# Second set-aside score of ordinary turns moved up by half a row, between two parts of a filling product

## The chip, the core and the metric

The kernel runs on one core of one Trainium2 chip. The metric is the device time of one execution in microseconds (us). Engines are named TensorE (PE, its weight loads PEld), VectorE (DVE), ScalarE (ACT), GpSimd (POOL) and SyncE (SP).

## The reference

One sequence of 2048 rows with 512 features is normalised by layer norm. From it come an attention with 32 heads of 16 and a feed-forward layer of width 1792 with squared ReLU; the output is the input plus the product of both, the second through a SiLU.

```python
xn = layernorm(x)                                # 2048 x 512
q, k, v = split(xn @ wqkv, 32 heads of 16)
p = softmax(q @ k.T / 4)                         # 32 x 2048 x 2048
s = (p @ v) @ wo
h = relu(xn @ w1 + b1) ** 2                      # 2048 x 1792
g = silu(h @ w2 + b2)
out = x + s * g
```

All of it is wanted in float32 accuracy.

## The kernel before

After a start of about 150 us, in which the rows are normalised and queries, keys and values are made, the kernel runs 128 *turns* of much the same shape, and then a short tail. A turn handles four steps; a step is four heads, 512 queries and 128 keys. Its work per step:

- scores: for each pair of heads `p` two products of 64 contraction rows, which lie on rows 0 to 63 (*half 0*, `hp` = 0) and 64 to 127 (*half 1*, `hp` = 1) of TensorE. The two halves work side by side, into different banks of PSUM.
- the exponential of the scores by ScalarE (`exps`, L286), from PSUM into an SBUF tile P.
- `values` (L538): P times the values, 16 products of 32 columns for a turn, all at the end of the turn.

The scores of three of the four steps go into one of two buffers S of two banks each (`scores`), and ScalarE reads them there. The fourth step, `i + 3`, has no such buffer: each of its four scores goes alone into a single bank, `single` (tile name `lin`), VectorE copies it to P (`aside`, L305), and ScalarE takes the exponential in place in P later. These are the four *set-aside scores* of a turn. They come as `aside(i + 3, 0, 0)`, `(0, 1)`, `(1, 0)` and `(1, 1)`; the first and third lie on half 0, the second and fourth on half 1. There is one bank for all of them.

Between the scores TensorE is given *filling products*, the matrices of the feed-forward layer and, in the last sixteen turns, of the projection `wo`. A `Block` (tile name `spare`, L330) is a sum of twelve (at the end some of nine) products in each half, with a list `todo` for each half and a counter `at`. A pair of blocks is worked on at a time: in a turn one block gets the rows of half 0 and the other those of half 1, and `swap` exchanges them, so that a block is done after two turns. `lin(0, 1)` issues the next filling product of both halves, `lin(0)` or `lin(1)` that of one half; the latter stand beside a set-aside score, which occupies the other half. Eight of the 128 turns make and end a pair of blocks in one turn (`make and end`) and have an order of their own. The other 120 are the *ordinary* turns.

The order on each engine is written out by hand in the loop over turns (L754 on); there is no scheduler. In an ordinary turn TensorE is given: S scores; score 1 beside a filling product of half 1; S scores; four filling products on both halves; score 2 beside a filling product of half 0; S scores; two filling products on both; S scores; score 3 beside one of half 1; two on both; S scores of the next turn's first step; two on both; score 4 beside one of half 0; S scores; the products of `values`. All products before `values` have 512 columns.

Of the kernel before, what the change touches and what calls it, by code (L numbers as in the profile page):

```python
# [73 lines left out]
def fast_path(tc, sb, ps, env):  # L74
# [6 lines left out]
    mm = nc.tensor.matmul  # L81
# [4 lines left out]
    def t(shape, dt, tag):  # L86

        cnt[0] += 1
        p = ps if tag in ("S", "lin", "acc") else sb
        if tag in BUFS:  # L90
            turn[tag] = turn.get(tag, -1) + 1
            n = turn[tag] % BUFS[tag]
            tag = f"{tag}{places[n] if tag == 'S' else n}"
        return p.tile(shape, dt, tag=tag, name=f"{tag}_{cnt[0]}")
# [183 lines left out]
    def score(i, p, hp, dst):  # L278
        qd, qc, kb = steps[i]
        k, q = ka[qd, kb // 8], qa[qd, qc]  # L280
        r = slice(64 * hp, 64 * hp + 64)
        mm(dst, k[r, p, 128 * (kb % 8):128 * (kb % 8) + 128], q[r, p], start=True, stop=True)  # L282

    def exps(i, p, src):
        if src is not None:
            act.activation(ptile[i, p], src, AF.Exp, scale=SCALE)  # L286

    def place(i, p):
        ptile[i, p] = t([128, 2, 512], FT, f"P{2 * ((i - 1) % 4) + p}")

    def scores(i, p):

        if i < len(steps):
            sc = t([128, 2, 512], FT, "S")
            place(i, p)
            for hp in range(2):
                score(i, p, hp, sc[:, hp])
            return sc

    def aside(i, p, hp):  # L300

        if hp == 0:
            place(i, p)
        score(i, p, hp, single)
        dve.tensor_copy(ptile[i, p][:, hp], single)  # L305
# [5 lines left out]
    class Block:  # L311
# [10 lines left out]
        def issue(self, half, bank):  # L322
# [8 lines left out]
               stop=n == len(self.todo[half]) - 1 and self.at[other] > 0)  # L331
            return True

    pair, swapped = [None], [0]

    def lin(*halves):
        if pair[0]:  # L340
            for half in halves:
                j = half ^ swapped[0]
                pair[0][j].issue(half, lin_banks[j])

    def swap():
        if pair[0]:
            while any([pair[0][half ^ swapped[0]].issue(half, lin_banks[half ^ swapped[0]]) for half in range(2)]):
                pass
            swapped[0] ^= 1
            if not swapped[0]:  # L350
                pair[0][0].evict()
                pair[0] = None
# [21 lines left out]
    def split_piece(eng=None):  # L374
        if at_piece[1] == len(pieces):
            return
        j, layer, m = pieces[at_piece[1]]
        at_piece[1] += 1
        raw, q = raws.pop(0), PAIRS[m][1]
        wf[layer, m] = [t([128, 4, 256] if layer == 1 else [128, 2, 512], FR, f"wf{layer}{p}{q}") for p in "hl"]  # L380
        split(*wf[layer, m], raw, eng or dve, pool)
        load_piece()
# [15 lines left out]
    def second(c, g, i):  # L398
        ms = [m for m in range(len(PAIRS)) if PAIRS[m][0] == g]
        h, w = [hid[m] for m in ms], [wf[2, m] for m in ms]  # L400

        def evict():
            if g == 0:
                y[c, i] = t([128, 2, 512], FT, f"y{i}")
            old = b2b.unsqueeze(1).broadcast_to([128, 2, 512]) if g == 0 else y[c, i]
            dve.tensor_tensor(y[c, i], spare, old, op=OP.add)
            if g == 3:
                complete.add((c, i))

        return [Block(lambda p, k, j=j: h[k // 2][p][:, k % 2, 128 * j:128 * j + 128],  # L410
                      lambda p, k: w[k // 2][p][:, k % 2], range(2 * len(ms)), evict)
                for j in (2 * i, 2 * i + 1)]
# [8 lines left out]
    for c in ORDER:  # L421
        for m, (g, _) in enumerate(PAIRS):
            fill += [(lambda m=m: first(m), False), (None, True)]
            if m in (1, 2, 4, 6):
                for i in range(2):
                    make = lambda c=c, g=g if m > 1 else 0, i=i: second(c, g, i)
# [9 lines left out]
    for i in range(4):  # L436
        part = vt[:, 4 * i:4 * i + 4]
# [94 lines left out]
    def values(i):  # L532
        qd, qc, kb = steps[i]
        if kb == 0:
            acc[0] = t([128, 512], FT, "acc")
        for j in (1, 2, 3, 0) if i % 2 else (0, 1, 2, 3):
            o = (4 * qd + j) * 17
            mm(acc[0][32 * j:32 * j + 32], vt[:, kb, o:o + 32], ptile[i, j // 2][:, j % 2],  # L538
               start=kb == 0, stop=kb == NK - 1)

    def finish(i):

        qd, qc, kb = steps[i]
        if kb < NK - 1:
            return
        if i == len(steps) - 1:
            return
        ou = t([128, 512], FT, "ou")
        cast(act if turn_ends_first[0] else dve, ou, acc[0])
        sp.dma_start(zdram[qd][qc], ou[16::32])  # L550
        for j in range(4):
            sp.dma_start(udram[qd // 2][qc][0, qd % 2, :, j], ou[32 * j:32 * j + 16])
        n = i // 4
        events.setdefault(2 * n + 2, []).insert(0, (load_sums, (qd, qc)))
        at(n + 2, rowsums, qd, qc)
# [174 lines left out]
    def happen(time):  # L730
        for fn, a in events.pop(int(2 * time), ()):
            fn(*a)


    n = turn["S"]
# [3 lines left out]
    lin_banks = [spare[:, 0], spare[:, 1]]  # L739
# [3 lines left out]
    def rest(i, dst):  # L743

        group(dst, lambda p: onorm[2, 3][p][:, cut[i]], lambda p: wos[0][p][:, 3])

    def end_rest(i, src):

        o = t([128, 512], FT, f"wf2{'hl'[i // 2]}{i % 2}")
        dve.scalar_tensor_tensor(o, src, 0.5, gsb[2, i // 2][:, i % 2], op0=OP.mult, op1=OP.mult)  # L750
        pool.dma_start(out[1024 + 128 * i:1152 + 128 * i], o, accum_op=OP.add)

    turn_ends_first = [False]
    for n in range(TURNS):  # L754
        i = 4 * n
        happen(n)
        make, end, split_now = fill[n]
        if make:
            pair[0] = make()
        exps(i + 1, 0, scores(i + 1, 0))  # L760
        aside(i + 3, 0, 0)
        lin(1)
        exps(i + 1, 1, scores(i + 1, 1))
        for _ in range(5 if make and end else 4):
            lin(0, 1)
        if make and end:
            lin(0)
            aside(i + 3, 0, 1)
            exps(i + 2, 0, scores(i + 2, 0))
            swap()  # L770
            exps(i + 2, 1, scores(i + 2, 1))
            aside(i + 3, 1, 0)
            lin(1)
            exps(i + 3, 0, ptile[i + 3, 0])
            lin(0, 1)
            last = [scores(i + 4, 0)]
            for _ in range(4):
                lin(0, 1)
        else:
            lin(0)  # L780
            aside(i + 3, 0, 1)
            exps(i + 2, 0, scores(i + 2, 0))
            lin(0, 1)
            lin(0, 1)
            exps(i + 2, 1, scores(i + 2, 1))
            aside(i + 3, 1, 0)
            lin(1)
            exps(i + 3, 0, ptile[i + 3, 0])
            lin(0, 1)
            lin(0, 1)  # L790
            last = [scores(i + 4, 0)]
            lin(0, 1)
            lin(0, 1)
        lin(0)
        aside(i + 3, 1, 1)
        exps(i + 3, 1, ptile[i + 3, 1])
        last.append(scores(i + 4, 1))
        for p in range(2):
            exps(i + 4, p, last[p])
        if n == TURNS - 1:  # L800
            two = t([128, 2, 512], FT, "S")
            rest(0, two[:, 0])
        turn_ends_first[0] = n < LAST and end and fill[n][0] is None and fill[n - 1][2] and n % per in (7, 15, 23)
        swap()
        if n == LAST - 1:
            gsb.update({(2, i): y[2, i] for i in range(2)})
        if n == TURNS - 1:
            end_rest(0, two[:, 0])
        happen(n + 0.5)
        if split_now:  # L810
            split_piece()
        for j in range(4):
            values(i + j)
        finish(i + 3)
# [5 lines left out]
    zc, r = t([128, 16], FT, "zc"), t([128, 16], FT, "rc")  # L820
# [3 lines left out]
    half = [slice(0, 256), slice(256, 512)]  # L824
# [11 lines left out]
    for i in range(4):  # L836
        for j in range(4):
            mm(small[32 * j:32 * j + 32, 0, cut[i]], r[:, 4 * i + j:4 * i + j + 1].broadcast_to([128, 32]), ident,
               start=True, stop=True)
# [19 lines left out]
    for j in range(2):  # L859
        for todo in ((0, 0), (0, 1)), ((1, 0),):  # L860
            for i in (2 * j, 2 * j + 1):
                group(lins[i], lambda p: (h, l)[p][:, cut[i]], lambda p: wlast[0][:, p],
                      start=len(todo) == 2, stop=len(todo) == 1, todo=todo)
# [120 lines left out]
```

## Time and profile before

| | us |
|---|---|
| median of 3 runs | 1272.64 (1272.08 to 1272.99) |
| profiled execution, its own time | 1271.87 |
| span of the profile | 1270.1 |
| TensorE busy | 1257.2 |
| ScalarE busy | 1034.1 |
| VectorE busy | 678.0 |

The granted clock of TensorE is 0.997 over the span. In the rows, L282 is the score's product (tiles S or lin), L286 the exponential, L305 VectorE's copy of a set-aside score, L330 a filling product, L538 the product with the values. "64*128 64x512" is a product of 64 rows into 128 columns of TensorE, 512 columns long. A weight load (PEld) stands as an instruction of its own before each product. The recorded ends of products are modelled, so distances between starts say more than durations.

### The profile page before, as it was taken

What the parts mean: (1) busy time and instruction counts of PE and PEld (TensorE: products, weight loads), DVE (VectorE), ACT (ScalarE), POOL (GpSimd) and SP (SyncE); (2) the same over time, 40 slices, a digit from 0 to 9 for tenths busy, and PEclk for the clock granted to TensorE, in tenths of its full rate; (3) what the DMA queues carried; (4) which work ended last, traced back from release to release, by engine and by line L of the source; (5) the groups of instructions that cost most, each with busy time, mean ns of one, the idle gap of its engine ahead of it and who ended that gap; (6) DMA issues with size and microseconds to landing.
All of it is one profiled execution on the core that took longest, in us unless ns stands there. A gap on an engine that the chain in (4) does not pass through costs nothing.

```text
span 1270.1 us, 24789 instructions
## 1 busy us (share of the span) xinstructions
PE 1257.2 (99%) x9925; PEld 720.9 (57%) x9925; DVE 678.0 (53%) x1064; ACT 1034.1 (81%) x1123; POOL 259.1 (20%) x150
## 2 busy tenths in 40 slices
PE   9999999999999999999999999999999999999997
PEld 7888755555555455555555555555555555545553
DVE  5542255455555554545465455555554545566655
ACT  4222588889899898898988889899889989998883
POOL 5000122122211221312022221220331212322112
PEclk9999999999999999999999999999999999999998
DMA  7565513132233232121423222333222122463445
GB/s 269 206 230 203 211 45 101 58 93 60 76 125 109 60 107 61 43 88 48 152 73 109 60 76 60 93 125 104 55 66 86 50 88 59 142 216 123 145 130 118
DMA packets 84940, 137.32 MB, mean 108 GB/s; under 512 B 26058, under 2 KB 40408, under 8 KB 83284
## 3 DMA queue, kind: packets, MB, share of 16 engines
q1 hardware_dynamic: 81668, 126.25, 30.4%
q0 software_dynamic: 2720, 8.65, 2.4%
q8 instruction: 79, 1.29, 0.4%
q10 hardware_dynamic: 432, 0.79, 0.2%
q14 instruction: 41, 0.34, 0.1%
HBM read 94.24 MB, written 41.41 MB: 107 GB/s over the span
## 4 chain that ended last, share of the span: by engine, by line
PE 96%; DVE 2%; ACT 1%; POOL 0%; DMA 0%; issue 0%; ACTq 0%; DVEq 0%
PE acc L538 36%; PE spare L330 26%; PE S L282 16%; PE S L111 9%; PE lin L282 7%; DVE P L305 1%; PE S L204 1%; POOL hl L104 0%; DMA P<-in_A_x_dram 0%; PE acc L111 0%; DVE st L166 0%; ACT P L286 0%; ACT wf2h L98 0%; PE spare L664 0%; DVE T L186 0%
## 5 line engine op out<-in xcount | busy, mean ns | idle before, releaser
L286 ACT ACTIVATE P<-S 128x1024 f32<-128x1024 f32 x768 | 732.5, 1021 | 67.8 <-PE S L282 64.4
L305 DVE COPY P<-lin 128x512 f32<-128x512 f32 x512 | 354.1, 692 | 467.6 <-PE lin L282 338.3
L538 PE MATMUL acc<-P,vt 128*32 128x512 f32 x4096 | 466.0, 595 | 0.0
L282 PE MATMUL S<-QA,KA 64*128 64x512 f32 x1536 | 332.6, 422 | 0.1
L286 ACT ACTIVATE P<-P 128x1024 f32<-128x1024 f32 x256 | 271.5, 1061 | 43.7 <-DVE P L305 43.5
L538 PEld LDWEIGHTS acc<-P,vt 128*32 128x32 f32 x4096 | 120.0, 109 | 272.9 <-issue 272.9
L282 PEld LDWEIGHTS S<-QA,KA 64*128 64x128 f32 x1536 | 145.0, 183 | 160.3 <-ACT P L286 142.9
L282 PE MATMUL lin<-QA,KA 64*128 64x512 f32 x512 | 213.0, 416 | 1.0 <-DVE P L305 0.5
L104 POOL TENSOR_TENSOR wf1l<-wr,wf1h 128x1024 fp32r<-128x1024 f32 x28 | 66.8, 2385 | 404.4 <-DVE wf1h L100 135.2
L330 PE MATMUL spare<-xl,wf1h 64*128 64x512 f32 x504 | 122.4, 400 | 0.0
L104 POOL TENSOR_TENSOR hl<-T,hh 128x1024 fp32r<-128x1024 f32 x28 | 67.6, 2416 | 242.2 <-DVE hh L100 139.6
L104 POOL TENSOR_TENSOR wf2l<-wr,wf2h 128x1024 fp32r<-128x1024 f32 x28 | 66.7, 2384 | 207.3 <-PE acc L538 139.0
L330 PE MATMUL spare<-wf2l,hh 64*128 64x512 f32 x448 | 106.8, 398 | 0.0
L282 PEld LDWEIGHTS lin<-QA,KA 64*128 64x128 f32 x512 | 94.1, 184 | 22.3 <-DVE P L305 14.0
L330 PE MATMUL spare<-xh,wf1l 64*128 64x512 f32 x504 | 96.1, 392 | 0.0
L330 PE MATMUL spare<-xh,wf1h 64*128 64x512 f32 x504 | 95.5, 390 | 0.0
L330 PE MATMUL spare<-wf2h,hh 64*128 64x512 f32 x448 | 87.6, 391 | 0.0
L330 PE MATMUL spare<-wf2h,hl 64*128 64x512 f32 x448 | 84.5, 390 | 0.0
L330 PEld LDWEIGHTS spare<-xl,wf1h 64*128 64x128 f32 x504 | 67.0, 184 | 8.4
L330 PEld LDWEIGHTS spare<-xh,wf1h 64*128 64x128 f32 x504 | 59.7, 184 | 9.9
L330 PEld LDWEIGHTS spare<-xh,wf1l 64*128 64x128 f32 x504 | 59.7, 185 | 8.6
L98 ACT CAST P<-S 128x512 fp32r<-128x512 f32 x30 | 17.6, 587 | 57.6 <-PE S L111 55.9
(202 smaller groups left out, 996.5 us busy)
## 6 DMA issues: line engine op xcount, KB each, us to landing
wr<-in_B_w_dram SPq DMA_DIRECT2D x56, 512.0 KB
KA<-kd SPq DMA_DIRECT2D x64, 256.0 KB
QA<-qd SPq DMA_DIRECT2D x128, 128.0 KB
kd<-P SPq DMA_DIRECT2D x15, 512.0 KB
qd<-P SPq DMA_DIRECT2D x15, 512.0 KB
u<-ud SPq DMA_DIRECT2D x15, 512.0 KB
P<-in_A_x_dram SPq DMA_DIRECT2D x8, 512.0 KB
xd<-KA SPq DMA_DIRECT2D x4, 1024.0 KB
```

The source lines that it names most:

```text
L98: act.copy(dst, src)
L104: leng.tensor_tensor(lo, src, hi.bitcast(FT), op=OP.subtract)
L111: mm(dst, lhs(a, k), rhs(b, k), start=n == 0, stop=n == len(todo) - 1)
L204: nc.tensor.transpose(pt[:, k, 128 * j:128 * j + 128], xnorm[c, i][:, j, 128 * k:128 * k + 128], ident)
L282: mm(dst, k[r, p, 128 * (kb % 8):128 * (kb % 8) + 128], q[r, p], start=True, stop=True)
L286: act.activation(ptile[i, p], src, AF.Exp, scale=SCALE)
L305: dve.tensor_copy(ptile[i, p][:, hp], single)
L330: mm(bank, self.lhs(a, k)[r], self.rhs(b, k)[r], start=n == 0 and self.at[other] == 0, stop=n == len(self.todo[half]) - 1 and self.at[othe ...
L538: mm(acc[0][32 * j:32 * j + 32], vt[:, kb, o:o + 32], ptile[i, j // 2][:, j % 2], start=kb == 0, stop=kb == NK - 1)
```

## The change

In ordinary turns the four filling products on both halves ahead of score 2 become three. Then half 0 gets its fourth product, and half 1 only the first 256 columns of its own fourth (`lin_part(1, 0)`). Score 2 follows. After it half 0 gets its fifth product (before, that one was issued ahead of score 2), and half 1 the last 256 columns of its fourth (`lin_part(1, 1)`). The two parts have the same weights and write the two halves of the same bank row; the counter moves on with the second. The turn has one product and one weight load more; nothing moves on VectorE, ScalarE, GpSimd or SyncE. The eight turns that make and end a pair keep their order.

```diff
+        def issue_part(self, half, bank, part):
+
+            n = self.at[half]
+            if n >= len(self.todo[half]):
+                return
+            assert 0 < n < len(self.todo[half]) - 1
+            k, a, b = self.todo[half][n]
+            r, c = slice(64 * half, 64 * half + 64), slice(256 * part, 256 * part + 256)
+            self.at[half] += part
+            mm(bank[:, c], self.lhs(a, k)[r], self.rhs(b, k)[r, c], start=False, stop=False)
+
...
+    def lin_part(half, part):
+        if pair[0]:
+            j = half ^ swapped[0]
+            pair[0][j].issue_part(half, lin_banks[j], part)
...
         aside(i + 3, 0, 0)
         lin(1)
         exps(i + 1, 1, scores(i + 1, 1))
-        for _ in range(5 if make and end else 4):
+        for _ in range(5 if make and end else 3):
             lin(0, 1)
         if make and end:
             lin(0)
...
         else:
+
             lin(0)
+            lin_part(1, 0)
             aside(i + 3, 0, 1)
+            lin(0)
+            lin_part(1, 1)
             exps(i + 2, 0, scores(i + 2, 0))
             lin(0, 1)
             lin(0, 1)
```

## Prediction

> **What bounds the kernel now.** I read the page first: the busy table, the costliest groups, the chain that ended last.
>
> ```profile
> span 1270.1 us, 24789 instructions
> PE 1257.2 (99%) x9925; PEld 720.9 (57%) x9925; DVE 678.0 (53%) x1064; ACT 1034.1 (81%) x1123; POOL 259.1 (20%) x150
> PE 96%; DVE 2%; ACT 1%; POOL 0%; DMA 0%; issue 0%; ACTq 0%; DVEq 0%
> L282 PEld LDWEIGHTS lin<-QA,KA 64*128 64x128 f32 x512 | 94.1, 184 | 22.3 <-DVE P L305 14.0
> ```
>
> TensorE is never idle for long, but a busy TensorE is partly a waiting one: the last row says that weight loads of the set-aside scores (tile lin) wait for VectorE's copies (L305). A turn has four set-aside scores, and all four use one bank, so each can start only when VectorE has copied the one before. The view of waits gives ScalarE's side of the turn:
>
> ```profile
> PEld S L282 <- ACT P L286: 142.9, 278, 0.8
> ACT P L286 <- PE S L282: 64.4, 109, 0.9
> ```
>
> Scores into the S banks wait 278 times for an exponential to free a bank; and 109 times, at 64.4 / 109 = 0.59 us each, ScalarE waits for scores, which is the start of a turn that runs as planned. Eight of the 109 are turns that the change leaves alone (those that make and end a block), so I count 101 turns for it.
>
> Next, the timeline of one such turn, engine by engine (start, duration; "x2" is both row halves of TensorE). TensorE's products:
>
> ```profile
> 503.56 0.39 PE L282 MATMUL lin<-QA,KA 64*128 64x512 f32 x1
> 504.72 0.38 PE L330 MATMUL spare<-xl,wf1h 64*128 64x512 f32 x1
> 504.94 0.39 PE L282 MATMUL lin<-QA,KA 64*128 64x512 f32 x1
> 504.94 0.39 PE L330 MATMUL spare<-xl,wf1h 64*128 64x512 f32 x1
> 505.17 0.39 PE L282 MATMUL S<-QA,KA 64*128 64x512 f32 x2
> 505.40 0.62 PE L330 MATMUL spare<-xl,wf1h 64*128 64x512 f32 x4
> 506.15 0.49 PE L282 MATMUL lin<-QA,KA 64*128 64x512 f32 x1
> 506.95 0.40 PE L282 MATMUL S<-QA,KA 64*128 64x512 f32 x2
> 507.65 0.39 PE L282 MATMUL lin<-QA,KA 64*128 64x512 f32 x1
> 507.88 0.40 PE L282 MATMUL S<-QA,KA 64*128 64x512 f32 x2
> 512.12 0.39 PE L282 MATMUL lin<-QA,KA 64*128 64x512 f32 x1
> ```
>
> The turn takes 512.12 - 503.56 = 8.56 us. A slot (a 512-column product on each row half at once) takes 0.23 us (504.94 to 505.17 to 505.40). The weight loads and the copies of the set-aside scores:
>
> ```profile
> 504.80 0.18 PEld L282 LDWEIGHTS lin<-QA,KA 64*128 64x128 f32 x1
> 505.81 0.19 PEld L282 LDWEIGHTS S<-QA,KA 64*128 64x128 f32 x2 [0.22 <-ACT P L286]
> 506.15 0.18 PEld L282 LDWEIGHTS lin<-QA,KA 64*128 64x128 f32 x1 [0.15 <-DVE P L305]
> 506.26 0.42 PEld L330 LDWEIGHTS spare<-xh,wf1l 64*128 64x128 f32 x3
> 506.75 0.19 PEld L282 LDWEIGHTS S<-QA,KA 64*128 64x128 f32 x2
> 504.05 0.69 DVE L305 COPY P<-lin 128x512 f32<-128x512 f32 x1 [1.88 <-PE lin L282]
> 505.40 0.69 DVE L305 COPY P<-lin 128x512 f32<-128x512 f32 x1 [0.66 <-PE spare L330]
> 506.75 0.69 DVE L305 COPY P<-lin 128x512 f32<-128x512 f32 x1 [0.66 <-ACT P L286]
> ```
>
> Copy 1 ends at 504.05 + 0.69 = 504.74, and 0.06 later score 2 loads its weights; copy 2 ends at 506.09, and 0.06 later score 3 loads. When a load is let go on waiting rows, the next load follows 0.11 later (506.15 to 506.26): that is when the product really starts. So score 3 really starts at 506.26, though its slot was due at 506.15 at the latest (505.92, when the S product released at 505.81 starts, plus 0.23). 0.11 us are lost there in every such turn. Score 2 loses nothing: its load (504.80) leads its slot (504.94) by 0.14, where 0.11 would do.
>
> ScalarE, the same turn (a row that merges two gives the first start and the last end):
>
> ```profile
> 504.74 1.96 ACT L286 ACTIVATE P<-S 128x1024 f32<-128x1024 f32 x2
> 505.67 1.94 ACT L286 ACTIVATE P<-S 128x1024 f32<-128x1024 f32 x2
> ```
>
> The third exponential of the turn starts at 505.67, which is 0.50 after its scores (505.17), and ends at 506.70; 0.05 later, at 506.75, the scores that reuse its bank load. Their slot is 506.95, a lead of 0.20. This lead is the reserve on which the forecast turns.
>
> **The change part by part.** It touches rows 64-127 (half 1) in the stretch from 504.72. Before: a whole filling product, score 2, S. After: half a product (256 columns), score 2, the other half, S. Rows 0-63 (half 0) keep their products; only one of them, the fifth, is now queued behind score 2's wait.
>
> *Score 2 moves, but not by half a row.* It would be due 0.12 earlier, at about 504.84, but its load still waits for copy 1 until 504.80, and the product starts 0.11 after that, at 504.91. A row shows what is won when score 2 is really let go by its load:
>
> ```profile
> 1150.59 0.18 PEld L282 LDWEIGHTS lin<-QA,KA 64*128 64x128 f32 x1 [0.21 <-DVE P L305]
> 1150.65 0.43 PE L282 MATMUL S<-QA,KA 64*128 64x512 f32 x1
> 1150.93 0.39 PE L282 MATMUL S<-QA,KA 64*128 64x512 f32 x1
> 1151.12 0.69 DVE L305 COPY P<-lin 128x512 f32<-128x512 f32 x1 [0.59 <-PE lin L282]
> ```
>
> There the copy starts 0.53 after the load; in the turn above it is 505.40 - 504.80 = 0.60. So copy 2, and with it score 3, comes 0.03 (504.94 - 504.91) to 0.07 earlier. The same rows show that the two halves need not run in step: half 0's S product starts 0.28 before half 1's, beside the score on half 1.
>
> *The queue behind the wait.* Half 0's fifth product can load only once score 2's load is released, 504.80; it is ready at 504.91 and due at 504.94. No cost; the cover is 0.03.
>
> *The cut product.* Columns are the same, but there is one weight load and one product more on half 1. A whole product is 0.23 a slot; half its columns are 0.11 to 0.12. The load of 128 columns must now fit under such a half. Its nearest row:
>
> ```profile
> 1253.36 1.05 PEld L831 LDWEIGHTS lin<-ident,P 128*128 128x128 f32 x8
> ```
>
> Eight loads in front of 4-column products: (1.05 - 0.19) / 7 = 0.12 each, so 0.12 per half product; lower bound 0.11, upper bound a whole slot, 0.23. I take 0.12, since the row is the same kind of load at the shortest distance the trace has. The Trainium skill (TensorE: Matmul & The Clock Gate, LDWEIGHTS) puts a load at columns / 1.2 GHz, an estimate of 0.107 us here; by it S below would come 0.01 earlier. No row of this trace has a 256-column product.
>
> *What S pays.* Half 1 stands still from 504.84 to 504.91, then score 2 takes 0.23 (505.14) and the second half 0.12: half 1's S product starts at 505.26 instead of 505.17, 0.09 later. The exponential needs both halves: it starts 0.50 later, 505.76 instead of 505.67, and ScalarE waits 0.09. Its end moves to 506.79, the load of the next S scores from 506.75 to 506.84, and the product starts 0.11 later at the earliest, 506.95. A row for that lead, from a turn in which ScalarE is late: the load at 377.26 is followed by its product at 377.37.
>
> ```profile
> 377.26 0.19 PEld L282 LDWEIGHTS S<-QA,KA 64*128 64x128 f32 x2 [0.16 <-ACT P L286]
> 377.37 0.41 PE L282 MATMUL S<-QA,KA 64*128 64x512 f32 x2
> ```
>
> 506.95 is when these scores start today. The next S scores, 507.88, follow it by 0.93 as before: the fourth exponential moves to an end of 507.61 + 0.09 = 507.70, plus 0.05 and 0.11 is 507.86, not late.
>
> *The sum.* TensorE reaches score 3 0.03 to 0.07 earlier, and gives it back three slots later to ScalarE: per turn 506.95 - 506.95 = 0.00. The uncertain terms are the load's lead (0.10 to 0.12) and the half product (0.11 to 0.13): 0.02 either way, times 101 turns 2.0 us either way. The eight make-and-end turns, the start and the tail are not touched; DMA queues, POOL and SP keep their order. The profiled execution took 1271.9 us (span 1270.1 and 1.8 around it), the median is 1272.64; a change of zero is put on the median: 1272.6, own range 1270.6 to 1274.6. About 0.2% (2.5 us) is what a measurement of this kernel can tell from no change.
>
> **The rivals.**
>
> *Faster: ScalarE does not follow.* If half 1's S product starts no later than about 505.20 (a quicker score and halves without the extra swap), the lead of 0.20 covers it, and score 3's advance stays: up to 0.06 x 101 = 6.1 us, 1266.5. For it: 0.09 is worked out from hundredths, and every 0.01 less is 1 us won. Against: half 1 has the same columns plus a standstill that the load at 504.80 fixes. Chance 0.25, most of it short of the full 6 us.
>
> *Slower: the exponential's wait outgrows the reserve.* Same place, other side: once half 1's S product starts later than 505.26, each further 0.01 costs 1 us. If a half product holds its rows for 0.17, midway between 0.12 and a whole slot, S starts 0.05 later: 5.1 us, 1277.7; with whole slots 505.37, 11 us, 1283.7. For it: two short products in a row half have never been seen here, and the recorded load (0.18 us) is longer than half a product. Against: loads follow each other at 0.12 in the row above. Chance 0.23.
>
> *Slower by more: loads that do not overlap.* If the load of a row half could not run beside that half's own product, half 1 would go 504.83 (half done), 504.94 (score 2 loaded), 505.15, 505.26 (loaded), 505.37, 505.48 (S): 0.31 late, less the 0.09 of reserve, 0.22 x 101 = 22 us, 1294.8. Against it, the slots of today: 0.23 a slot has no room for 0.21 of columns and 0.11 of load one after the other. The Trainium skill (same page, Part 3, The mechanism) says that a load overlaps running products only when their row group differs, which speaks against cutting a product in two. By that rule the trace disagrees: the load at 504.80 lies beside half 1's product that began at 504.72. Chance 0.04.
>
> *The change hardly does what it says.* Score 2 moves by 0.03 to 0.07 and not by 0.12; that is already in the forecast.
>
> **How the numbers follow.** No measurable change 0.48, faster 0.25, slower 0.27 (0.23 and 0.04). The likeliest is the give-back: 1272.6. The range 1268.0 to 1277.0 holds that case, most of the faster one short of its full price, and the slower one up to 0.045 us a turn; what is left outside is about 0.2.
>
> **What the profile after would show.** Right: loads of score 2 still 0.06 after copy 1; copy 2 0.53 to 0.57 after that load; score 3's load about 1.29 to 1.32 after score 2's instead of 1.35; half 1's S product about 0.09 after half 0's; a new wait of some 0.09 of ScalarE for S in the middle of the turn; the S load that follows the third exponential leading its product by 0.11; turns of 8.56. Wrong: turns of 8.50 with S and ScalarE hardly later (faster), or 256-column products holding half 1 for clearly more than 0.12 (slower).

## The result and the profile after

The changed kernel takes 1269.88 us (median, 1269.32 to 1270.48); the kernel before, measured beside it, takes 1272.35 us. The ratio is 0.998, with a 95% interval of 0.9972 to 0.9987: 2.5 us faster, which is just the 0.2% that the prediction set as its bound. The profiled execution took 1270.20 us (span 1268.4) against 1271.87 (span 1270.1) for the profile before. The number of products and of weight loads grew by 120, one for each ordinary turn:

```profile
span 1268.4 us, 25029 instructions
PE 1255.2 (99%) x10045; PEld 715.0 (56%) x10045; DVE 677.9 (53%) x1064; ACT 1041.5 (82%) x1123; POOL 259.0 (20%) x150
PE 95%; DVE 2%; ACT 1%; issue 1%; POOL 0%; DMA 0%; ACTq 0%; DVEq 0%
L282 PEld LDWEIGHTS lin<-QA,KA 64*128 64x128 f32 x512 | 94.1, 184 | 29.7 <-DVE P L305 6.7
```

In the view of waits the loads of S scores wait for ScalarE about as long in all as before (142.9 us, 278 times), and ScalarE for S scores too:

```profile
PEld S L282 <- ACT P L286: 144.4, 286, 0.8
ACT P L286 <- PE S L282: 64.7, 110, 0.9
```

These totals hide that the place of the wait has moved. For the counts here and below I take the ordinary turns under 8.6 us in the kernel before, 102 of the 119 that another turn follows, and call them *planned*. A wait in this view is a longer idle stretch of the weight loads that an exponential ends. In the middle of a planned turn of the kernel before it stands ahead of the S load after the second exponential (505.81 in the prediction's turn) in all 102, and ahead of the one after the third (506.75) in none. In the changed kernel it stands ahead of the one after the third in all 102 (506.24 below), and ahead of the one after the second (505.23 below) in 13.

The same turn as in the prediction, from the changed kernel (it begins with score 1 at 502.97, L343 is the cut product):

```profile
502.97 0.39 PE L282 MATMUL lin<-QA,KA 64*128 64x512 f32 x1
504.12 0.28 PE L343 MATMUL spare<-xl,wf1h 64*128 64x256 f32 x1
504.24 0.47 PE L282 MATMUL lin<-QA,KA 64*128 64x512 f32 x1
504.55 0.28 PE L343 MATMUL spare<-xl,wf1h 64*128 64x256 f32 x1
504.59 0.47 PE L282 MATMUL S<-QA,KA 64*128 64x512 f32 x2
511.50 0.39 PE L282 MATMUL lin<-QA,KA 64*128 64x512 f32 x1
504.21 0.18 PEld L282 LDWEIGHTS lin<-QA,KA 64*128 64x128 f32 x1
504.32 0.19 PEld L343 LDWEIGHTS spare<-xl,wf1h 64*128 64x128 f32 x1
505.23 0.19 PEld L282 LDWEIGHTS S<-QA,KA 64*128 64x128 f32 x2
505.49 0.18 PEld L282 LDWEIGHTS lin<-QA,KA 64*128 64x128 f32 x1
505.61 0.41 PEld L330 LDWEIGHTS spare<-xh,wf1l 64*128 64x128 f32 x3
506.24 0.19 PEld L282 LDWEIGHTS S<-QA,KA 64*128 64x128 f32 x2 [0.21 <-ACT P L286]
506.34 0.65 PEld L330 LDWEIGHTS spare<-xh,wf1l 64*128 64x128 f32 x5
504.75 0.69 DVE L305 COPY P<-lin 128x512 f32<-128x512 f32 x1 [0.59 <-PE lin L282]
505.16 1.03 ACT L286 ACTIVATE P<-S 128x1024 f32<-128x1024 f32 x1
```

Score 2's load is at 504.21, 1.24 after score 1, exactly where it was (504.80 - 503.56). The product really starts 0.11 later, where the next load of its half stands (504.32). Copy 2 follows the load by 0.54 instead of 0.60, so score 3's load comes 505.49 - 502.97 = 2.52 after score 1 instead of 2.59: 0.07 won. Its product, read in the same way from the next load, really starts at 2.64 (505.61) instead of 2.70 (506.26). In the middle of the turn the two S products (504.59, x2) no longer start together: half 1's is recorded 0.08 after half 0's (median of the planned turns; 0.01 in the kernel before). The third exponential starts 2.19 after score 1 instead of 2.11, the S load that it frees 3.27 instead of 3.19, and its product 3.37 (506.34, where the next load stands) instead of 3.39. The medians of the planned turns, 2.12 to 2.19 for the third exponential and 3.20 to 3.27 for the S load, put this delay at 0.07. The turn takes 511.50 - 502.97 = 8.53 instead of 8.56. The median planned turn went from 8.55 to 8.53, and the planned turns are shorter by 1.96 us in the sum.

### The profile page after: what moved, and what is told of

It is laid out like the page before. It is cut to its first block, busy times and chain, and to the rows that moved or that the text cites. A ratio compares the mean times of both kernels' runs of the same rounds, so it can differ in the third digit from the quotient of the medians.

```text
span 1268.4 us, 25029 instructions
## 1 busy us (share of the span) xinstructions
PE 1255.2 (99%) x10045; PEld 715.0 (56%) x10045; DVE 677.9 (53%) x1064; ACT 1041.5 (82%) x1123; POOL 259.0 (20%) x150
## 4 chain that ended last, share of the span: by engine, by line
PE 95%; DVE 2%; ACT 1%; issue 1%; POOL 0%; DMA 0%; ACTq 0%; DVEq 0%
PE acc L554 36%; PE spare L330 24%; PE S L282 16%; PE S L111 9%; PE lin L282 8%; PE spare L343 1%; ACT P L286 1%; DVE P L305 1%; PE S L204 1%; POOL hl L104 0%; DMA P<-in_A_x_dram 0%; PE acc L111 0%; DVE st L166 0%; ACT wf2h L98 0%; PE spare L680 0%
## 5 line engine op out<-in xcount | busy, mean ns | idle before, releaser
L282 PE MATMUL S<-QA,KA 64*128 64x512 f32 x1536 | 344.1, 424 | 0.3
L282 PEld LDWEIGHTS S<-QA,KA 64*128 64x128 f32 x1536 | 163.8, 183 | 180.0 <-ACT P L286 144.4
L330 PE MATMUL spare<-xl,wf1h 64*128 64x512 f32 x440 | 109.1, 392 | 0.0
L330 PE MATMUL spare<-wf2l,hh 64*128 64x512 f32 x400 | 95.6, 391 | 0.0
L330 PEld LDWEIGHTS spare<-xl,wf1h 64*128 64x128 f32 x440 | 62.2, 184 | 0.8
```

The lines of the kernel that those rows point to most:

```text
L330: mm(bank, self.lhs(a, k)[r], self.rhs(b, k)[r], start=n == 0 and self.at[other] == 0, stop=n == len(self.todo[half]) - 1 and self.at[othe ...
```

## The experiments

Theory A is the prediction's: two chains decide a turn. VectorE's copy lets score 2 go, and what is won there arrives at score 3; but half 1's S product comes later, the third exponential after it, and the bank that this frees takes most of the gain back. Theory B: only the order of products on TensorE, and the cut itself, count.

**Cut at column 128.** Score 2 is moved up by three quarters of a row.

```diff
-            r, c = slice(64 * half, 64 * half + 64), slice(256 * part, 256 * part + 256)
+            r, c = slice(64 * half, 64 * half + 64), (slice(0, 128), slice(128, 512))[part]
```

> The changed kernel, but cut at column 128: half 1 gets 128 columns ahead of score 2 and 384 behind it. Theory A (score 2 is let go by VectorE's copy, and what is won at score 3 is given back through half 1's S product, the third exponential and the bank it frees): score 2 still starts 0.11 after its load at 1.24 (times from score 1 of the turn), half 1 stands still 0.06 longer ahead of it, its S product moves from 1.70 to about 1.76, the third exponential from 2.19 to 2.25, the turn gets 0.05 to 0.06 longer: 1275 to 1276 us, against 1269.9 of the changed kernel and 1272.4 of the kernel before. Theory B (what counts is only that TensorE does the same products in another order, with one load more): the same products, loads and order as in the changed kernel, 1269.9 us.

Measured: 1276.01 us, ratio 1.003 (1.0019 to 1.0041). The turn that begins with score 1 at 504.89:

```profile
506.14 0.18 PEld L282 LDWEIGHTS lin<-QA,KA 64*128 64x128 f32 x1
507.13 1.03 ACT L286 ACTIVATE P<-S 128x1024 f32<-128x1024 f32 x1
508.21 0.19 PEld L282 LDWEIGHTS S<-QA,KA 64*128 64x128 f32 x2 [0.22 <-ACT P L286]
```

Score 2's load has not moved (1.25); the third exponential is at 2.24, 0.05 after that of the changed kernel, and the S load at 3.32. Half 1 only stands still longer. The median planned turn is 0.06 longer than in the changed kernel, as theory A has it; theory B is out.

**S ahead of the second part.** The cut is kept; only the order of the second part and the S scores is exchanged.

```diff
             lin(0)
-            lin_part(1, 1)
             exps(i + 2, 0, scores(i + 2, 0))
+            lin_part(1, 1)
             lin(0, 1)
```

> The changed kernel, but the second part of the cut product comes behind the S scores instead of ahead of them. Theory A: score 2 as early as in the changed kernel, half 1's S product back at about 1.63 from 1.70, the third exponential back at 2.12, the S load behind it back at 3.20, so that score 3's advance of 0.06 stays: turns of 8.50 us, 1266 to 1268 us. Theory B: 1269.9 us, as the changed kernel.

Measured: 1264.86 us, ratio 0.9942 (0.9928 to 0.9955). The turn that begins with score 1 at 501.37:

```profile
501.37 0.39 PE L282 MATMUL lin<-QA,KA 64*128 64x512 f32 x1
502.61 0.18 PEld L282 LDWEIGHTS lin<-QA,KA 64*128 64x128 f32 x1
503.88 0.18 PEld L282 LDWEIGHTS lin<-QA,KA 64*128 64x128 f32 x1
504.56 0.18 PEld L282 LDWEIGHTS S<-QA,KA 64*128 64x128 f32 x2
503.49 1.03 ACT L286 ACTIVATE P<-S 128x1024 f32<-128x1024 f32 x1
509.84 0.39 PE L282 MATMUL lin<-QA,KA 64*128 64x512 f32 x1
```

Scores 2 and 3 load at 1.24 and 2.51, as in the changed kernel. The third exponential is back at 2.12 and the S load at 3.19, and the turn is 8.47. The give-back is gone and the whole advance of score 3 stays; the median planned turn is 0.062 below that of the kernel before, 6.6 us in the sum. The wait for ScalarE ahead of the S load after the third exponential is seen in 32 planned turns instead of 102. The measured gain of 7.5 us is somewhat more than the turns hold, and the time lies below the 1266 to 1268 expected. This kernel beats both.

**The cut alone.** Both parts ahead of score 2, which has its old place.

```diff
             lin(0)
             lin_part(1, 0)
-            aside(i + 3, 0, 1)
-            lin(0)
             lin_part(1, 1)
+            lin(0)
+            aside(i + 3, 0, 1)
             exps(i + 2, 0, scores(i + 2, 0))
```

> The changed kernel, but both parts of the cut product ahead of score 2, as the whole one stood before: only the cut is left of the change. Theory A: score 2 in its old place or 0.01 to 0.02 later, copies as before, so nothing is won at score 3 and the extra load costs at most 0.015 a turn: 1272.4 to 1274 us. Theory B (the cut product itself is what pays, for example by giving loads more room): 1269.9 us.

Measured: 1271.64 us, ratio 0.9994 (0.9985 to 1.0003), no measurable change; the median planned turn is 8.556 us, against 8.554 in the kernel before. The cut neither pays nor costs; the place of score 2 does. The expectation's own cost of 0 to 1.6 us did not show.

**Shorter copies in the kernel before.** VectorE copies 256 columns of each set-aside score and fills the rest with a constant afterwards, so half of these scores is left out.

```diff
-        dve.tensor_copy(ptile[i, p][:, hp], single)
+        dve.tensor_copy(ptile[i, p][:, hp, :256], single[:, :256])
+        dve.memset(ptile[i, p][:, hp, 256:], 0.5)
```

> The kernel before, but VectorE copies only 256 of the 512 columns of a set-aside score and fills the others with a constant afterwards, so that TensorE is let go earlier; half of these scores is left out of the result. Theory A: scores 2 and 3 no longer wait for a copy; score 3 starts in its slot at about 2.59 instead of 2.69, then the S load freed by the third exponential (3.20 + 0.11) is next: turns 0.07 to 0.08 shorter, 1264 to 1265.5 us. Theory B (score 3's wait is not what the turn pays for): 1272 us.

Measured: 1262.54 us, ratio 0.9924 (0.991 to 0.9937). The copies, and the waits of the loads for ScalarE:

```profile
501.00 0.42 DVE L305 COPY P<-lin 128x256 f32<-128x256 f32 x1 [1.95 <-PE lin L282]
502.75 0.19 PEld L282 LDWEIGHTS S<-QA,KA 64*128 64x128 f32 x2 [0.20 <-ACT P L286]
502.86 0.19 PEld L282 LDWEIGHTS lin<-QA,KA 64*128 64x128 f32 x1
503.10 0.18 PEld L331 LDWEIGHTS spare<-xh,wf1l 64*128 64x128 f32 x1
PEld S L282 <- ACT P L286: 179.0, 471, 0.8
```

A copy takes 0.42 instead of 0.69. Score 3's load (502.86) now follows the S load at once and waits for no copy; the product starts where the next load stands, 503.10, which is 2.60 after score 1 at 500.50, against 2.70 (506.26 - 503.56) before. The median planned turn is 0.083 shorter, 8.4 us in the sum. So the wait for VectorE's copies is what the turn pays for, and this is what its removal is worth, until ScalarE sets the pace: the loads of S scores then wait for ScalarE 471 times instead of 278, and the one after the third exponential does so in 101 of the 102 planned turns instead of none. The time lies 1.5 us below the 1264 to 1265.5 expected: the median turn gained slightly more than the 0.07 to 0.08 forecast, and about 1.1 us more came from ordinary turns that are not planned ones. The eight turns that make and end a pair gained nothing.

**Shorter copies in the changed kernel.** The same edit there.

> The changed kernel with VectorE's copies cut to 256 of 512 columns, the rest filled with a constant afterwards (as in the run with short copies of the kernel before; half of the set-aside scores is left out). Theory A: with the copies out of the way the cut product and its place win nothing more: score 2 in its new slot at 1.28, no standstill, half 1's S product at 1.64, turns within 0.01 of those of the kernel before with short copies, 1262 to 1264 us. Theory B (the order itself is worth 2.5 us): 1260 us.

Measured: 1262.47 us, ratio 0.9919 (0.9905 to 0.9932), the same as the run before within 0.1 us. Its loads wait for ScalarE nearly as often as there:

```profile
PEld S L282 <- ACT P L286: 174.8, 451, 0.8
```

With the copies out of the way the new place of score 2 wins nothing more. Both kernels with short copies meet the same limit, the S load after the third exponential (3.20 after score 1 in both), so this run alone does not exclude a small gain by another way. Together with the rows of the changed kernel, where copy 2 and score 3's load come 0.07 earlier, it fits that the change wins through the copies.

**Cut at column 384.** What does a short product cost its half?

```diff
-            r, c = slice(64 * half, 64 * half + 64), slice(256 * part, 256 * part + 256)
+            r, c = slice(64 * half, 64 * half + 64), (slice(0, 384), slice(384, 512))[part]
```

> The changed kernel, but cut at column 384: 384 columns ahead of score 2, 128 behind it, S after both as in the changed kernel. It measures what a short product holds its rows for. If the load behind it is the bound (0.11 to 0.12 whatever the columns): half 1 stands still only 0.01 ahead of score 2, but its S product comes at 1.35 + 0.23 + 0.11 = 1.69 to 1.70 as in the changed kernel, 1269 to 1270 us. If a short product costs its columns and the swap (0.05 + 0.01): S at 1.64, the third exponential hardly later than before the change, turns of 8.49, 1265 to 1266 us.

Measured: 1269.16 us, ratio 0.9973 (0.9964 to 0.9983). The turn that begins with score 1 at 502.69:

```profile
504.03 0.40 PE L282 MATMUL lin<-QA,KA 64*128 64x512 f32 x1
504.04 0.19 PEld L343 LDWEIGHTS spare<-xl,wf1h 64*128 64x128 f32 x1
504.27 0.22 PE L343 MATMUL spare<-xl,wf1h 64*128 64x128 f32 x1
504.30 0.47 PE L282 MATMUL S<-QA,KA 64*128 64x512 f32 x2
504.87 1.03 ACT L286 ACTIVATE P<-S 128x1024 f32<-128x1024 f32 x1
```

Half 1 has hardly a standstill left ahead of score 2 (504.03 is 1.34 after score 1), yet the third exponential is at 2.18, 0.01 ahead of the changed kernel's 2.19, and not at 2.12. Half 1's S load stands at 1.58 in both kernels (median), when the short product starts, and its product can really start only 0.11 later: a product of 128 columns holds its half as long as one of 256. Neither of the other two places of the cut, 128 and 384, gives a measurable gain over 256 in this order.

**A whole row.** No cut: half 1's fourth product goes behind score 2 and the S scores.

```diff
             lin(0)
-            lin_part(1, 0)
             aside(i + 3, 0, 1)
             lin(0)
-            lin_part(1, 1)
             exps(i + 2, 0, scores(i + 2, 0))
+            lin(1)
             lin(0, 1)
```

> No cut: half 1's whole fourth product is moved behind score 2 and the S scores, so that score 2 is moved up by a whole row. Theory A: score 2 starts no earlier than in the changed kernel (its load waits for copy 1 at 1.24), so half 1 only stands still, 0.2 instead of 0.07, and stays 0.13 further behind half 0; S on time at 1.63 and score 3 at 2.63 to 2.76, so what the kernel with S ahead of the second part wins is lost again: 1271 to 1277 us. If an earlier place is worth something by itself: 1265 us or less.

Measured: 1275.58 us, ratio 1.0024 (1.0015 to 1.0033). The turn that begins with score 1 at 504.85:

```profile
506.09 0.50 PE L282 MATMUL lin<-QA,KA 64*128 64x512 f32 x1
507.17 0.59 PE L282 MATMUL S<-QA,KA 64*128 64x512 f32 x2
507.45 0.42 PE L282 MATMUL lin<-QA,KA 64*128 64x512 f32 x1
```

Score 2 stands in the row at 1.24, its load's time; scores go no earlier than in the changed kernel. Half 1 runs a further 0.11 behind: the two products of the second S pair (507.17) are recorded 0.19 apart, against 0.08 in the changed kernel (medians of the planned turns). Score 3, on half 0, is as early as in the changed kernel (2.60); but score 4 lies on half 1 and comes late (4.13 after score 1 against 4.09 in the kernel before, medians), and the median planned turn is 0.04 longer than before. ScalarE does not set this: the S load after the third exponential waits for it in one planned turn. So half a row is better than a whole one, not because score 2 moves by it (copy 2 starts only 0.06 to 0.07 earlier in both), but because a whole row leaves half 1 behind.

## Why the prediction was right

Its steps, one by one, from the rows above. *Score 2 moves less than half a row*: right, its load stayed at 1.24. *Copy 2 0.53 to 0.57 after the load*: 0.54. *Score 3 0.03 to 0.07 earlier*: 0.07, the upper end. *The fifth product of half 0 queued behind the wait costs nothing*: right, half 0's S product stayed in its place. *A half product costs 0.12*: the standstill, score and second half together put half 1's S 0.08 behind half 0's where 0.09 was forecast; the run cut at column 384 puts the hold of a short product at 0.11. *The exponential and the S load behind it*: 2.19 and 3.27, where 2.20 and 3.28 were forecast. The new wait of ScalarE is too short for the view of waits (110 against 109); it shows in the starts of the second and third exponential, 1.00 apart instead of 0.93 (medians). *The give-back*: right in mechanism; the wait for ScalarE moved to the S load after the third exponential in every planned turn, the run with S ahead of the second part removes just this link and keeps the gain, and the run cut at column 128 lengthens it and loses.

The sum was slightly off. The forecast put the freed S product at 3.39, in its old place, and the change at 0.00 a turn; it came at 3.37, and the turn gained 0.019. The terms that were mis-sized are the ones worked out from hundredths: the S product's delay (0.08, not 0.09) and the lead of the load before its product (0.10, not 0.11). On a reserve used up to the last hundredth this decided between "no change" and 2.5 us: the measured 1269.88 lies within the stated range of 1268.0 to 1277.0, but 0.7 below the likeliest case's own range, so that the likeliest case, no measurable change, was narrowly missed. The time is four tenths of the way to the faster rival's 6.1 us, but that rival's mechanism did not come: it wanted half 1's S product at most 0.03 late and ScalarE in its old place, and both came 0.07 to 0.08 late. That the time still fell within the stated range is owed in part to its width, which was made to hold most of the faster case. The rival that loads do not overlap products of their own half is out: it would have cost 22 us, and the cut alone costs nothing measurable. The slower rival did not come in the changed kernel, but its rule did: once half 1's S is later, each 0.01 costs about 1 us (the third exponential 0.06 later in the median with the cut at 128, 6.1 us more).

The measured gains are 0.5 to 1 us larger than the sums over the planned turns (2.5 against 1.96, and 7.5 against 6.6). Most of this is the difference between a profiled execution and a median. The profiles of the kernel before and of the changed one are only 1.67 us apart: the planned turns gained 1.96, and the other ordinary turns lost 0.33. The profile before happened to be 0.5 below the median of its kernel, that of the changed kernel 0.3 above its own. With S ahead of the second part the profiles are 7.18 apart, of which 0.5 lie behind the last turn's start. Why single executions of one kernel differ by such amounts is open.

## What to carry to other kernels

When a hand-off is moved up, follow both streams that pass the place: what the moved step wins on its own chain, and what the work behind it now delivers later to another engine, up to the next buffer that this engine frees. Here the second nearly ate the first, and exchanging two instructions (S ahead of the rest of the cut product) kept it: 7.5 us instead of 2.5. A step that waits for a semaphore moves only as far as the semaphore lets it; place beyond that is standstill.

## What was not expected of the hardware

The two row halves of TensorE ran out of step by 0.08 (the changed kernel) and by 0.19 (the whole row), and half 0 was not held up by it: score 3 on half 0 loads at 2.52 in both. A product's recorded start can lie ahead of the time at which it really begins: with the cut at column 384 half 1's S product is recorded 0.03 after half 0's (median of the planned turns), in the changed kernel 0.08, and yet the third exponential is only 0.01 earlier. The start of the next weight load on the same half tells the real time better, and it is how the starts of scores 2 and 3 were read here.
